# Retention attention into a gated two-layer product on one core: the last block's first product as seven products, in turns with the block before it

## The chip, the cores and the metric

The kernel runs on one core of a Trainium2 chip. The metric is the device time of one execution in microseconds, as a median over runs. The profile is one more execution, recorded by the hardware profiler. Its engines are TensorE (PE, with its weight loads shown apart as PEld), VectorE (DVE), ScalarE (ACT), GpSimd (POOL) and SyncE (SP), which here issues nearly all DMAs. TensorE writes to PSUM, which has eight banks of 2 KB per partition; the other results go to SBUF.

## What is computed

The first part is a causal attention without softmax, whose scores decay with distance by a factor of each head; the second is two matrix products with a gate between them. There are 8 batches, 8 heads, 576 positions, a head size of 64, a model width of 512 and an inner width of 2048:

```python
scores = scale * np.matmul(q, k.transpose(0, 1, 3, 2))
Dmat = np.where(rel >= 0, gamma[:, None, None] ** rel[None, :, :], 0.0)
x = np.matmul(scores * Dmat[None, :, :, :], v)   # then (batch, position) rows x 512
h = x @ w_in                                     # 4608 x 512 by 512 x 2048
g = h * (1.0 / (1.0 + np.exp(-beta * h)))        # beta: one value per inner column
out = g @ w_out                                  # 4608 x 2048 by 2048 x 512
```

## The kernel before

The 4608 rows are worked on in nine blocks of 512. Blocks 0 to 7 are the first 512 positions of each batch; block 8 collects the last 64 positions of the eight batches, the tails. The attention of a block leaves its rows turned in `xT` (width on the partitions). The first product (`up`, L761) makes one of 16 stripes of 128 inner columns with four matmuls of 128x512; ScalarE applies Silu with the column's `beta` to it out of PSUM. From block 3 on the odd stripes go through an f32 scratch (`hs`), and VectorE scales them by a ratio of betas (L773), so that two neighbouring stripes have the same scale. The sixteen stripes together are `gT`.

From block 3 on the second product is made by a scheme of seven products for a 2x2 splitting of both factors, instead of eight. The sums of `gT` quarters that it needs are made by VectorE (`seven_a`, L783: `sa`), in two halves of eight stripes; those of the weights were made once (`seven_b`). Each product and each half of the rows is one chain of eight matmuls of 128x256 (`seven_mm`, L794). The products run in the order 3, 4, 1, 5, 2, 7, 6 on three PSUM chains: U takes 3, then 2 and 6 on top; W takes 4, then 5; Z takes 1, then 7. What stands in a chain after each product is taken out at once (`seven_out`, L810): after 4, ScalarE copies W to c12 and VectorE adds U to it for c21; after 1, ScalarE copies Z to c22; after 5, ScalarE copies W to c11 and VectorE makes c12 = c21 - c11; after 2, VectorE subtracts U from c21; after 7, it adds Z to c11; after 6, U to c22. A product that is added to a chain must wait until the chain's last state has been read.

The order of work is written by hand, and each engine works through its own queue in the order in which the program issues instructions. `fill` is a list of steps, mostly TensorE's: for every block from 3 on 16 `up` and then 14 `seven_mm` (seven products, two halves of the rows). All other work (loads, preparation on POOL, turning by DMA, attention, sums) lies in `streams` of pairs (position, step). `merged` (L913) issues each of them just ahead of the fill entry with that number. `base[n]` is the number of block n's first entry; a position below is called a slot, counted from the block's start. The loop at L1101 places the sums `seven_a`, the loop at L1114 the attention: in the turn of block n the attention of block n + 1.

The tails' attention lies in the turn of block 7. `pair_prep` places its loads (`load_tail`), its preparation on POOL (`pre`) and its turning (`x_tail`, a transposing DMA on SP) by distances to two anchors. `tail_scores` (L701) is placed at slot 5, and `both_tails` (L754) at slot 13: it makes the outputs and then the parts that come from the states, behind a fence on ScalarE. The last step of the tails is `out` (L747): four times two casts of 128x256 on ScalarE from PSUM to block 8's `xT`, at slots 16.3 to 22.5.

PSUM tiles share their banks by tags: "mm" has three, "O" and "sc" two each, "st" one. The tiles of `up` take "mm" in turn, and so do the chains U and W; Z takes "O". Attention scores and outputs take "sc" and "O". For the last block each half of the rows has chains of its own (`alone`), which take further banks of "sc".

Of the kernel before, what the change touches and what calls it, by code (L numbers as in the profile page):

```python
# [19 lines left out]
def kernel(  # L20
# [10 lines left out]
    nc = tc.nc  # L31
# [703 lines left out]
    def tail_crosses(i0, later):  # L735

        O4, after = live[i0]["O4"]

        def cross(j, x, t, y, pp, after):
            p = 2 * y + pp  # L740
            mm(O4[x, y][row_d(j ^ y), pp, t, :], ends[2 * t + x][row_d(j), p, :], live[i0 + t]["qkT"][row_d(j), 0, p, half(x)],
               after=after)

        for own in range(2):
            paired(*[[F(cross, j, j ^ own, t, y, pp, after if own else None) for t in range(NT) for pp in range(2) for y in range(2)]
                     for j in range(2)])
        def out(x, y, O):  # L747
            for r in range(2):
                to = xt(B)[:, 2 * y:2 * y + 2].rearrange("k p (a r) (s l x) -> k (p a) r l x s", r=2, l=2, x=2)[:, :, r, :, x, :]
                nc.scalar.copy(to, O[:].rearrange("k p (a l) (r s) -> k (p a) r l s", l=2, r=2)[:, :, r])  # L750

        later += [F(out, x, y, O) for (x, y), O in O4.items()]
# [23 lines left out]

    def quarter(m, odd, second, ks):

        return gts[m][:, 2 * ks.start:2 * ks.stop].rearrange("f (k j) (p i) s -> f k j p i s", j=2, i=2)[:, :, odd, :, second]
# [14 lines left out]
    def seven_mm(m, j, p, alone):  # L794

        c, n = chain_of[j], p if alone else 0
        if j in (3, 4, 1) and (alone or p == 0):
            tag = {"U": ("mm", "mm"), "W": ("mm", "sc"), "Z": ("O", "sc")}[c][p] if alone else "O" if c == "Z" else "mm"
            chains[c, n] = psum.tile([P, 1 if alone else 2, NH], F32, name=c, tag=tag, bufs=dict(mm=3, O=2, sc=2)[tag])
        for k in range(KH):  # L800
            if j in (3, 4):
                a = gts[m][:, 2 * k + (j == 4), 2 * p + (j == 4), :]
            else:
                a = sums_a[0][:, held_in[j], k, p, :]
            nc.tensor.matmul(chains[c, n][:, 0 if alone else p], a, sevens[k // 2][:, j - 1, k % 2, :],  # L805
                             start=j in (3, 4, 1) and k == 0 and (alone or p == 0), stop=k == KH - 1, skip_group_check=True)
        if alone or p == 1:
            seven_out(m, j, slice(p, p + 1) if alone else slice(0, 2), n)
# [31 lines left out]
    def seven_store(m, a, ps, ns):  # L840

        for p in range(ps.start, ps.stop):
            if m < B:
                nc.sync.dma_start(out[m * S:m * S + MB].rearrange("(s i) n -> s i n", i=CB)[:, 2 * p + a, ns], ots[m][:, 2 * p + a, ns])
            else:
                rows = out.rearrange("(b s) n -> s b n", s=S)[MB + a * TL // 2:MB + (a + 1) * TL // 2, CB * p:CB * (p + 1), ns]
                nc.sync.dma_start(rows, ots[m][:, 2 * p + a, ns])

# [245 lines left out]
    lead[B - 1] = 5  # L1094
# [6 lines left out]
    for n in range(SB, B + 1):  # L1101
# [5 lines left out]
        else:  # L1107
            early = [t + 11.4, t + 12.6, t + 15.3, t + 15.4] if n == SB + 1 else [t + 9.8, t + 10.8, t + 11.8, t + 14.4] if n < B else span(t + 9, 4)
# [5 lines left out]
    for n in range(1, B):  # L1114
# [65 lines left out]
```

## Time and profile before

| What | us |
|---|---|
| median of 3 runs (lowest to highest) | 292.71 (291.99 to 292.92) |
| the profiled execution | 293.46 |
| its span, first to last instruction | 291.8 |
| block 7, first product, with the tails' scores and outputs | 234.04 to 249.91 |
| block 7, second product | 249.91 to 262.35 |
| block 8, first product | 262.35 to 275.95 |
| block 8, second product | 275.95 to 288.4 |
| last combination and stores | 288.4 to 291.8 |

All times inside the span are counted from its start. A row of a group or of a timeline names the line of the kernel, the engine, the operation, the tile written and the tiles read, and the shape; in square brackets stand the idle time of the engine ahead of it and what ended that. Matmuls overlap in TensorE's pipeline, so a matmul's own duration (273 ns for 256 columns) is longer than the distance between two of them.

### The profile page before, as it was taken

How to read it: one execution, taken by the hardware profiler on the slowest of the kernel's cores; microseconds unless marked ns; L12 is line 12 of the kernel's file. 1: busy time of each engine (PE TensorE's matmuls, PEld its weight loads, DVE VectorE, ACT ScalarE, POOL GpSimd, SP SyncE). 2: the span in 40 equal slices, each digit the busy share in tenths (PEclk: the TensorE clock that was granted, in tenths of full speed). 3: DMA queues.
4: the chain of work that ended last, by engine and by line, in shares of the span. 5: the costliest groups of instructions: out<-in, count | busy, mean ns of one | idle time of the engine just before them, and what ended most of it. 6: DMA issues, size and time to landing. Idle time of an engine off the chain costs nothing.

```text
span 291.8 us, 8653 instructions
## 1 busy us (share of the span) xinstructions
PE 280.2 (96%) x3599; PEld 177.4 (61%) x3627; DVE 187.6 (64%) x347; ACT 169.5 (58%) x298; POOL 133.0 (46%) x258
## 2 busy tenths in 40 slices
PE   7899999999999999999999899999999999999995
PEld 5674446764544455548845685578557855784584
DVE  5974545704795296299598794986498545642673
ACT  4377636686968873674157514762476156837730
POOL 6366029924980972678583593434079300000000
PEclk9999999999999999999999999999999999999999
DMA  7999999969999999999999928960678530003004
GB/s 223 309 365 385 380 306 283 189 127 239 186 196 284 222 163 260 283 234 162 255 258 182 246 62 231 175 141 2 205 163 171 81 146 3 0 24 122 0 3 143
DMA packets 120568, 54.05 MB, mean 185 GB/s; under 512 B 93889, under 2 KB 113361, under 8 KB 120529
## 3 DMA queue, kind: packets, MB, share of 16 engines
q1 hardware_dynamic: 120496, 53.49, 76.5%
q8 instruction: 28, 0.46, 0.6%
q14 instruction: 12, 0.09, 0.1%
q10 hardware_dynamic: 32, 0.01, 0.0%
HBM read 36.71 MB, written 9.44 MB: 158 GB/s over the span
## 4 chain that ended last, share of the span: by engine, by line
PE 88%; DVE 5%; DMA 3%; issue 2%; SPq 1%; ACT 0%; POOL 0%; DVEq 0%
PE ph L768 37%; PE po L893 14%; PE U L805 10%; PE Z L805 7%; PE W L805 6%; PE O L550 4%; PE ph L860 4%; DMA kvn<-in_k_dram 3%; PE sc L550 2%; DVE sa L789 2%; PE st L550 2%; DVE sbd L293 1%; PE ph L875 1%; DVE sum L586 1%; PE st L510 1%
## 5 line engine op out<-in xcount | busy, mean ns | idle before, releaser
L768 PE MATMUL ph<-xT,w_in_sb 128*128 128x512 bf16 (+1 forms) x542 | 114.2, 363 | 2.2 <-issue 0.6
L768 PEld LDWEIGHTS <-w_in_sb 128*128 128x128 bf16 x560 | 53.5, 98 | 56.1 <-DVE sum L586 0.9
L775 ACT ACTIVATE gT<-ph,beta_sb 128x512 bf16<-128x512 f32 (+1 forms) x92 | 58.3, 640 | 44.5 <-PE ph L768 43.5
L805 PEld LDWEIGHTS <-sa 128*128 128x128 bf16 x480 | 46.9, 98 | 6.3 <-issue 0.6
L773 DVE TENSOR_SCALAR gT<-hs,ratio 128x512 bf16<-128x512 f32 x48 | 25.8, 539 | 34.4 <-ACT hs L772 33.9
L789 DVE TENSOR_TENSOR sa<-gT 128x1024 bf16<-128x1024 bf16 (+1 forms) x54 | 44.5, 866 | 0.7 <-PE Z L805 0.4
L330 POOL TENSOR_TENSOR qs<-qn,gq 128x256 bf16<-128x256 f32 x48 | 31.9, 696 | 28.1 <-DMA qn<-in_q_dram 20.8
L772 ACT ACTIVATE hs<-ph,beta_sb 128x512 f32<-128x512 f32 x48 | 33.0, 687 | 20.0 <-PE ph L768 19.7
L893 PE MATMUL po<-w_out_sb,gT 128*128 128x512 bf16 x184 | 42.0, 379 | 1.0 <-issue 0.8
L312 POOL TENSOR_TENSOR vn<-kvn,gv 128x256 bf16<-128x256 f32 x48 | 33.3, 714 | 7.6 <-issue 3.2
L367 POOL CAST kn<-kvn 128x128 bf16<-128x128 f32 (+1 forms) x72 | 25.0, 383 | 17.2 <-DMA kvn<-in_k_dram 17.1
L893 PEld LDWEIGHTS <-gT 128*128 128x128 bf16 x192 | 18.1, 98 | 20.9
L805 PE MATMUL U<-b,sa 128*128 128x256 bf16 x192 | 22.9, 273 | 0.4 <-DVE ot L819 0.4
L805 PE MATMUL Z<-b,sa 128*128 128x256 bf16 x192 | 23.1, 273 | 0.0
L293 DVE TENSOR_TENSOR R<-sc,late 128x512 bf16<-128x512 f32 x24 | 15.4, 679 | 11.2 <-issue 10.0
L805 PEld LDWEIGHTS <-gT 128*128 128x128 bf16 x192 | 18.7, 98 | 3.5
L255 DVE TENSOR_TENSOR b<-wt 128x512 bf16<-128x512 f32 x20 | 15.9, 851 | 1.9 <-ACT wt L238 1.8
L448 DVE TENSOR_TENSOR R<-sc,causal 128x512 bf16<-128x512 f32 x16 | 10.2, 682 | 2.2 <-PE sc L550 2.0
L379 POOL CAST kn<-kvn 128x512 bf16<-128x512 f32 x6 | 3.8, 653 | 16.9 <-DMA kvn<-in_k_dram 16.9
L805 PE MATMUL W<-b,gT 128*128 128x256 bf16 x96 | 11.5, 273 | 0.0
L805 PE MATMUL W<-b,sa 128*128 128x256 bf16 x96 | 11.5, 273 | 0.0
L805 PE MATMUL U<-b,gT 128*128 128x256 bf16 x96 | 11.5, 273 | 0.0
(121 smaller groups left out, 316.7 us busy)
## 6 DMA issues: line engine op xcount, KB each, us to landing
qn<-in_q_dram SPq DMA_DIRECT2D x16, 512.0 KB, 5.6
out_dram<-ot SPq DMA_DIRECT2D x32, 256.0 KB, 3.2
wt<-in_moe_w_out_dram SPq DMA_DIRECT2D x8, 512.0 KB, 9.4
kvn<-in_k_dram SPq DMA_DIRECT2D x12, 256.0 KB, 6.6
kvn<-in_v_dram SPq DMA_DIRECT2D x12, 256.0 KB, 5.9
kvn<-in_k_dram SPq DMA_DIRECT2D x24, 128.0 KB, 4.7
kvn<-in_v_dram SPq DMA_DIRECT2D x24, 128.0 KB, 3.8
wt<-in_moe_w_in_dram SPq DMA_DIRECT2D x5, 512.0 KB, 8.3
```

The source lines that it names most:

```text
L293: return lambda: f(*a)
L312: nc.gpsimd.tensor_tensor(vn[:, hs], v[:, hs], g[:, hs], ALU.mult)
L330: nc.gpsimd.tensor_tensor(batch[b]["qs"][:, cs, to], q_tiles[b][:, hs, cs].rearrange("p h i d -> p i h d"), gq[:, cs, hs].unsqueeze(3).to_ ...
L367: nc.gpsimd.tensor_copy(kn[:, c % 2, to], t[:, 0, hs])
L550: ins = nc.tensor.matmul(out, lhsT, rhs, start=start, stop=stop, skip_group_check=True)
L768: nc.tensor.matmul(ph, w_in_sb[:, ko, fo * P:(fo + 1) * P], xts[m][:, ko, :, w], start=(ko == 0), stop=(ko == KO - 1))
L772: nc.scalar.activation(h, ph, ACT.Silu, scale=beta_sb[:, fo:fo + 1])
L773: nc.vector.tensor_scalar(gts[m][:, fo], h, ratio[:, fo // 2:fo // 2 + 1], None, ALU.mult)
L775: nc.scalar.activation(gts[m][:, fo, :, w], ph, ACT.Silu, scale=beta_sb[:, fo:fo + 1])
L789: nc.vector.tensor_tensor(sums_a[0][:, held_in[j], ks], quarter(m, *x, ks), quarter(m, *y, ks), op)
L805: nc.tensor.matmul(chains[c, n][:, 0 if alone else p], a, sevens[k // 2][:, j - 1, k % 2, :], start=j in (3, 4, 1) and k == 0 and (alone o ...
L893: nc.tensor.matmul(po[:, :nn], gT[:, fo, ms, :], w_out_sb[:, fo, n0:n0 + nn], start=(fo == 0), stop=(fo == FO - 1))
```

## The change

Block 8's sixteen `up` steps leave the fill list. Block 8's first product is now made by the same kind of scheme with seven products, transposed: the weights `w_in` are the operand that stays in TensorE, and the block's rows stream by. `w_sums` makes the five sums of weight quarters on POOL (20 steps of 128x512 bf16), in two halves from 11 slots before block 7's start on. `x_sums` makes the five sums and two negations of the rows' quarters at slots 10 to 16 of block 7, the sums on VectorE and the negations on ScalarE. `up_seven(g, j)` issues product j for group g (four of the sixteen stripes) in two halves `q`, four matmuls of 128x256, and then the same kind of combination as `seven_out`, on f32 tiles `cs` of 128x512. The chains are `chain8`: two U in the banks of "sc", one W in "st", one Z in "O". `swish8` applies Silu from those tiles; the odd stripes are scaled by POOL, or by VectorE in the last of the four groups.

`down_and_up(7)` takes the place of block 7's 14 `seven_mm` steps: each is split in two halves of four matmuls, and behind each of the first 24 halves stands one product of block 8 (two at the start of a group). Two halves with what stands behind them are one entry of `fill`, so the mixed stage has 14 entries, and `base[8]` counts as if 16 ended with them. The banks of two of the `alone` chains of block 8's second product change places.

The tails' scores move to slot 0.3, which is issued ahead of entry 1, their outputs to 5.6, their casts to 6.4, 6.5, 8.3 and 8.4, two of the four now on VectorE; their loads, preparation and turning move eight slots earlier with them. Block 8's sums `seven_a` are spread anew.

```diff
-        def out(x, y, O):
+        def out(n, x, y, O):
             for r in range(2):
                 to = xt(B)[:, 2 * y:2 * y + 2].rearrange("k p (a r) (s l x) -> k (p a) r l x s", r=2, l=2, x=2)[:, :, r, :, x, :]
-                nc.scalar.copy(to, O[:].rearrange("k p (a l) (r s) -> k (p a) r l s", l=2, r=2)[:, :, r])
+                e = nc.vector.tensor_copy if n % 2 else nc.scalar.copy
+                e(to, O[:].rearrange("k p (a l) (r s) -> k (p a) r l s", l=2, r=2)[:, :, r])
...
-    def seven_mm(m, j, p, alone):
+    def seven_mm(m, j, p, alone, ks=range(KH)):
...
-            tag = {"U": ("mm", "mm"), "W": ("mm", "sc"), "Z": ("O", "sc")}[c][p] if alone else "O" if c == "Z" else "mm"
+            tag = {"U": ("mm", "sc"), "W": ("mm", "mm"), "Z": ("O", "sc")}[c][p] if alone else "O" if c == "Z" else "mm"
...
+    def w_sums(ks):
+        w = w_in_sb[:].rearrange("p (r o) (k e f) -> p r o k e f", r=2, e=2, f=P)
+        cols = slice(ks.start * P, ks.stop * P)
+        def one(j):
+            if j not in ws:
+                ws[j] = stage.tile([P, KO // 2, KH * P], BF16, name="ws", tag="kvn", bufs=NQ)
...
+            for o in range(KO // 2):
+                to = ws[j][:, o, cols].rearrange("p (k f) -> p k f", f=P)
+                nc.gpsimd.tensor_tensor(to, *[w[:, r, o, ks, e] for e, r in (x, y)], op)
+        return [F(one, j) for j in (1, 5, 2, 7, 6)]
...
+    def up_seven(g, j):
+        c = chain_of[j]
+        if not chain8:
+            gts[B] = [stage.tile([P, KH, CB, P], BF16, name="g8", tag="qn", bufs=2) for _ in range(2)]
+            for k, tag, n in (("U0", "sc", 2), ("U1", "sc", 2), ("W", "st", 1), ("Z", "O", 2)):
+                chain8[k] = psum.tile([P, 2, 2 * P], F32, name="c8", tag=tag, bufs=n)
...
+        for q in range(2):
+            k = 2 * g + q
+            for o in range(KO // 2):
+                a = w[:, o if j == 3 else 2 + o, k, int(j == 4)] if j in (3, 4) else ws[j][:, o, k * P:(k + 1) * P]
+                nc.tensor.matmul(t[:, q], a, xs[j][:, o], start=j in (3, 4, 1) and q == 0 and o == 0, stop=o == KO // 2 - 1,
+                                 skip_group_check=True)
...
+        if j == 4:
+            nc.scalar.copy(c12, t)
+            nc.vector.tensor_tensor(c21, c12, chain8[f"U{g % 2}"][:].rearrange("f q (p s) -> f q p s", p=2), ALU.add)
+        elif j == 1:
+            nc.scalar.copy(c22, t)
+        elif j == 5:
+            nc.scalar.copy(c11, t)
+            nc.vector.tensor_tensor(c12, c21, c11, ALU.subtract)
+        elif j == 2:
+            nc.vector.tensor_tensor(c21, c21, t, ALU.subtract)
+        elif j == 7:
+            nc.vector.tensor_tensor(c11, c11, t, ALU.add)
+        elif j == 6:
+            nc.vector.tensor_tensor(c22, c22, t, ALU.add)
...
+        nc.scalar.activation(h, h, ACT.Silu, scale=beta_sb[:, fo:fo + 1])
+        by = nc.vector if g == WG - 1 else nc.gpsimd
+        by.tensor_scalar(gt(B, fo)[:, 0].rearrange("f i s -> f (i s)"), h, ratio[:, fo // 2:fo // 2 + 1], None, ALU.mult)
...
+    def down_and_up(m):
+        halves = [F(seven_mm, m, j, p, False, range(x * KH // 2, (x + 1) * KH // 2)) for j in seven for p in range(2) for x in range(2)]
+        units = [[f] for f in halves]
+        for g in range(WG):
+            for x, js in enumerate(((3, 4), (1,), (5,), (2,), (7,), (6,))):
+                units[6 * g + x] += [F(up_seven, g, j) for j in js]
+            for x, e, q in ((5, 0, 0), (6, 0, 1), (6, 1, 0), (7, 1, 1)):
+                units[6 * g + x].append(F(swish8, g, e, q))
...
-        base[n] = len(fill)
-        fill += [F(up, m, fo) for fo in range(FO)]
+        base[n] = len(fill) - (FO if m == B else 0)
+        fill += [F(up, m, fo) for fo in range(FO)] if m < B else []
+        if m == B - 1:
+            fill += down_and_up(m)
+            continue
...
-    lead[B - 1] = 5
+    lead[B - 1] = -3
...
+            if n == B:
+                order = [(t + 12, 5, first), (t + 13, 2, first), (t + 14.1, 7, first), (t + 16.1, 1, first)]
+                order += [(t + 16.8 + 0.1 * x, j, second) for x, j in enumerate((1, 5, 2, 7))] + [(t + 22.1, 6, first), (t + 22.2, 6, second)]
...
-            streams.append([(t0, F(tail_scores, take[0])), (t + 13, F(both_tails, take[0], outs))] +
-                           queued([t + 16.3, t + 17.6, t + 20.5, t + 22.5], outs))
+            streams.append([(t + 0.3, F(tail_scores, take[0])), (t + 5.6, F(both_tails, take[0], outs))] +
+                           queued([t + 6.4, t + 6.5, t + 8.3, t + 8.4], outs) +
+                           [(t + 10 + x, F(x_sums, j)) for x, j in enumerate((3, 4, 1, 5, 2, 7, 6))])
+            streams.append(queued(span(t - 11, 5, 2.4), w_sums(slice(0, KH // 2))) + queued(span(t + 2, 5, 2.4), w_sums(slice(KH // 2, KH))))
```

More of the change, by code (lines that the diff above doesn't have):

```diff
@@ new lines, in x_sums @@
+    def x_sums(j):
+        if not xs:
+            for n, tag in enumerate(("kn", "kn", "kT", "kT")):
+                t = sb.tile([P, 2, KO // 2, 2, P], BF16, name=tag, tag=tag, bufs=4)
+                xs.update({1 + 2 * n: t[:, 0], 2 + 2 * n: t[:, 1]})
+        x = xts[B][:].rearrange("k (r o) (p i) s -> k r i o p s", r=2, i=2)
+        b11, b12, b21, b22 = (x[:, r, i] for r in range(2) for i in range(2))
+        if j in (2, 5):
+            for o in range(KO // 2):
+                nc.scalar.activation(xs[j][:, o], (b11 if j == 2 else b22)[:, o], ACT.Copy, scale=-1.0)
+            return
+        l, r, op = {1: (b11, b22, ALU.add), 3: (b12, b22, ALU.subtract), 4: (b21, b11, ALU.subtract),
+                    6: (b11, b12, ALU.add), 7: (b21, b22, ALU.add)}[j]
+        nc.vector.tensor_tensor(xs[j], l, r, op)
@@ new lines, in swish8, with unit @@
+    def swish8(g, e, q):
+        fo, h = 4 * g + 2 * q + e, cs[g % 2][e][:, q]
+        if e == 0:
+            nc.scalar.activation(gt(B, fo)[:, 0].rearrange("f i s -> f (i s)"), h, ACT.Silu, scale=beta_sb[:, fo:fo + 1])
+            return
+        nc.scalar.activation(h, h, ACT.Silu, scale=beta_sb[:, fo:fo + 1])
[9 more added lines that the diff above has]
+                units[6 * g + x].append(F(swish8, g, e, q))
+        def unit(n):
+            for f in units[2 * n] + units[2 * n + 1]:
+                f()
+        return [F(unit, n) for n in range(len(units) // 2)]
```

28 lines of the change are left out of this document (22 added, 6 removed).

## The prediction

> **What bounds the kernel now.** I read the busy table first, then the chain that ended last, then the busy time by stages, and last the timelines of single engines around the last two blocks. Busy table, two lines of the chain, and four stages (columns: stretch, length, then busy time of PE, PEld, DVE, ACT, POOL with instruction counts, granted clock, DMA share, GB/s):
>
> ```profile
> PE 280.2 (96%) x3599; PEld 177.4 (61%) x3627; DVE 187.6 (64%) x347; ACT 169.5 (58%) x298; POOL 133.0 (46%) x258
> ...
> 250.07 1.75 PE U L805 x16
> ...
> 276.11 1.75 PE U L805 x16
> ...
> 160.50:162.50 2.00, 0.90 (x61) 0.68 (x50) 1.55 (x4) 0.00 (x0) 0.85 (x2) 1.00 0.63 97
> ...
> 234.04:249.91 15.87, 15.62 (x253) 7.82 (x255) 8.59 (x16) 10.46 (x16) 0.00 (x0) 1.00 0.17 64
> 249.91:262.35 12.44, 12.39 (x113) 11.06 (x113) 7.25 (x12) 7.13 (x13) 0.00 (x0) 1.00 0.02 8
> 262.35:275.95 13.60, 13.54 (x62) 6.17 (x63) 6.58 (x12) 10.28 (x15) 0.00 (x0) 1.00 0.19 71
> ```
>
> The reader is to see that TensorE (PE) sets the end: in the last three stages it never waits, while VectorE (DVE) is half idle and ScalarE (ACT) idles in the second product (7.13 of 12.44 us). So a change here gains only TensorE work, and loses wherever it makes TensorE wait. The prices of the other engines come from the timelines (start, length, engine, line, tiles, idle time before):
>
> ```profile
> 238.80 2.48 DVE L717 TENSOR_TENSOR R<-sc,tri 128x512 bf16<-128x512 f32 x4
> 251.35 2.50 DVE L789 TENSOR_TENSOR sa<-gT 128x1024 bf16<-128x1024 bf16 x4
> 262.34 0.69 DVE L833 TENSOR_TENSOR ot<-ot,U 128x512 f32<-128x512 f32 x1 [1.06 <-PE U L805]
> 250.11 0.69 ACT L772 ACTIVATE hs<-ph,beta_sb 128x512 f32<-128x512 f32 x1 [0.18 <-PE ph L768]
> 250.70 2.44 ACT L750 CAST xT<-O 128x256 bf16<-128x256 f32 x4
> 255.35 0.59 ACT L821 COPY ot<-Z 128x512 f32<-128x512 f32 x1
> 255.83 1.31 ACT L750 CAST xT<-O 128x256 bf16<-128x256 f32 x2
> 164.26 5.80 DVE L789 TENSOR_TENSOR sa<-gT 128x1024 bf16<-128x1024 bf16 x6
> 170.71 1.91 PE L805 MATMUL U<-b,sa 128*128 128x256 bf16 x16 [0.43 <-DVE ot L819]
> ```
>
> To see here: a Silu takes 0.69 us, but the next ScalarE step starts 0.59 behind it; a 128x512 copy takes 0.59 and frees the engine after 0.48; an output cast of the tails costs 0.61 to 0.65; a VectorE combination out of PSUM 0.69 (0.62 in a row: the four masks); a sum of 128x1024 costs 0.62 in a row. The last two lines are block 4: six sums in a row kept VectorE for 5.80 us, the read of U stood behind them, and TensorE waited 0.43. That is how this change can lose.
>
> **The change part by part.**
>
> *TensorE.* From the U chain of block 7 to that of block 8 (250.07 to 276.11) are 26.04 us. A seven-product chain of 16 matmuls takes 1.747 (starts 249.91, 251.66, 253.40), so 109.2 ns for 256 columns and 12.23 us for block 7's 112. The other 13.81 us are block 8's 64 matmuls of 512 columns, 215.8 ns each. Removed: 64 x 0.2158 = 13.81. Added: 4 groups x 7 products x 4 = 112 matmuls of 256 columns x 0.1092 = 12.23. Gain 1.58 us; the mixed stage then needs 24.46 of pure TensorE time.
>
> *Tail attention eight slots earlier* (scores from slot 5 to slot 1 of block 7, outputs from 13 to 6; a slot is one entry of the fill list). TensorE does the same 0.67 + 1.56 us. Scores end at 235.6, the four masks 2.48 later at 238.1; outputs come at 239.9: no wait. All else of the tails moves along: 24 loads and 4 transposes on SP, 32 POOL steps. On SP the first tail's six loads (189.52 to 194.4, 4.9 us) now stand ahead of the last key transpose of batch 7, whose scores run at about 206, with 3.4 us to land: hidden by some 8 us, and up to 4.9 without that. The second tail's loads pass block 5's first stores, which wait on VectorE until 204 anyway: nothing. The last transposes, issued until 227.9 before, move to about 221, for scores at 234.9. POOL ends the tails by about 222 instead of 228.8; the last tail's values there may wait for batch 7's outputs (217.5), with only the new weight sums queued behind. Each of these is costed at nothing.
>
> *Weight sums on POOL.* 20 steps of 128x512. No row has bf16 operands; the nearest is the value scaling of 128x512 at 1.04 us, bounds 0.65 (the cast of that size) and 1.81 (two of 128x256 at 0.906). At 1.04: 222 to 243; at 1.81: 258. The first ten are wanted at 253 and are done by 240 even then, the second at about 265: hidden. The upper end would slow block 7's sums beside it (six at 0.97 while POOL worked, against 0.62), some 1.4 us.
>
> *ScalarE in block 7's first product.* Block 7's 16 Silus now share their stage with four of the eight output casts, which before lay in ScalarE's free time, and four negations (0.3 each: half of the 0.62 of a 128x512 negation). Walk with 0.863 us per `up`: `up` 6 ends at 242.31; Silu 6, two casts, Silu 7 at 244.17, Silu 8 at 244.77, two casts, Silu 9 at 246.63, ready 247.32. Three PSUM buffers serve the `ph` tiles, so `up` 12 needs that one: due at 246.63, it starts at 247.37. **0.75 us lost.** Bounds: 0 if casts cost 0.37 (a plain 128x256 copy), 1.3 if no two steps overlap. I take 0.75, by the rows of the same casts. The stage ends at T = 250.82; the last Silu starts at T + 0.6.
>
> *The mixed stage.* Per group (g) ScalarE has four Silus and three copies (4 x 0.59 + 3 x 0.48 = 3.8 us), VectorE five combinations (3.3), TensorE 6.12: by totals all fits. Four groups and block 7's own 5 combinations and sums take VectorE to about 24 of 24.5, so it is the order that decides. First group: VectorE ends block 7's first-product work and the input sums at T + 2.7, reads U for c21 until 3.4, then has block 7's four second-half sums (2.5) in front of c12 = c21 - c11 (to 6.5) and c21 -= U (to 7.15). TensorE wants to add product 6 into U at T + 5.25 and starts at 7.2: **1.95 lost** (bounds 1.35, if the input sums are done early, and 2.6, if every step takes its full length). For the next groups the loop is: VectorE c11 += Z; ScalarE four Silus, then copies c12, block 7's own, c22, c11, queued behind the Silu that waits; VectorE c12 and c21. That is 4 x 0.6 + 4 x 0.5 + 0.1 and three times 0.65: 6.5 us against 6.12. In group 2 (and 3, 4) I get waits of **0.85, 1.2 and 0.6** at product 6; group 3 has block 7's sum of 128x2048 (1.23) in its way, group 4 two first-half sums of block 8. Together 2.65; bounds 0 (loop below 6.12) and 4.7 (the same walk with every step at full length).
>
> *Block 8's second product.* TensorE has T + 29.1 for its first chain, 30.85 for its second (W), whose PSUM buffer is that of block 7's U. That is read last by block 7's c22 += U, which stands on VectorE behind two multiplications that wait for the last Silus and one sum: done at 32.5. **1.7 lost**; after it sums and chains keep up. Bounds 0.5 (Silus 1.2 earlier) and 2.5.
>
> *Nothing* I put on the rest: stores, the halves of chains (same matmuls), and the multiplications that go to POOL. The last are 0.65 to 1.04 each, in the 6.5 us of a group, and are wanted two groups later; if they fell beside c12, that one would take 1.10 (172.12, POOL busy) instead of 0.69.
>
> Sum: -1.58 + 0.75 + 1.95 + 2.65 + 1.7 = +5.5 us. The profiled execution took 293.46 (span 291.8 and 1.66 around it), 0.75 above the median of the three runs, 292.71; it would come to 298.9, the median to **298.2**. All low ends together +0.3 (293.0), all high ends +9.5 (302.2).
>
> **Rivals.**
>
> *Evictions keep up* (other side). Place: the read of U before product 6 of each group; price: all waits go, 292.71 - 1.58 = 291.1. It decides where the group loop falls below 6.12 us and the first group's chain ends by T + 5.25. For: no second product of blocks 5 to 7 waits, and totals fit. Against: the first chain holds 2.5 us of sums that no overlap shortens. If only some of the waits go, the gain and they cancel: 291.8 to 293.6, no change.
>
> *The change doesn't save TensorE time.* Every 256 columns need a weight load of 98 ns, inside 109; with two streams in turns, a load not taken ahead at a switch would cost 98 ns, 56 switches 5.5 us: 303.7. Against: U, W and Z chains follow each other now with other tiles and banks at an even 1.747.
>
> *The clock drops.* The waits come in every group. In block 4 TensorE stood still for 0.94 us and the stretch from 160.50 kept the clock at 1.00. If the clock halved for one group's 56 matmuls, that is 6.1 us more, 304.3. The Trainium skill, page TensorE: Matmul & The Clock Gate, section "A second HAM failure mode: psum-queue depth-cycling", says that short idle gaps between groups as banks are cycled can throttle the clock. The trace shows no such thing; its gaps were fewer than those I expect.
>
> **How the numbers follow.** The forecast 0.74 (293.6 to 302.2); evictions keep up 0.13; waits and gain cancel 0.05; no TensorE saving 0.05; clock 0.03. The point is the forecast's, 298.2. The range leaves out the faster case, the clock and half of the unsaved time (0.19): 292.0 to 302.2; the forecast's own is 293.6 to 302.2. A measurement of this kernel tells about 0.3% (0.9 us) from no change: faster 0.13, same 0.05, slower 0.82.
>
> **What would show it.** The matmul work of the last two blocks falls by about 1.6 us, at 109 ns a step within groups. Block 7's first product takes about 16.8 us instead of 15.9, its late Silus back to back. TensorE waits for VectorE's subtraction from U before each product 6, first for about 2 us; the mixed stage takes 29.1. A wait of about 1.7 us for block 7's last combination stands before block 8's W chain. POOL's sums end by about 243, and the clock stays 1.00. I am wrong if the mixed stage takes under 26 us, if VectorE's four sums do not stand between c21 and c12, or if TensorE waits for POOL or a transpose.

## The result and the profile after

The changed kernel takes 303.05 us (median of six runs, 301.82 to 304.15); the kernel before took 292.46 beside it (291.99 to 293.05). The ratio is 1.034 with a 95% interval of 1.032 to 1.037: slower, by nearly twice what was forecast, and just above the range. The profiled execution took 302.85 with a span of 300.8, so the spans are 9.0 us apart. The medians are 10.6 apart: the profiled execution of before (293.46) is 1.0 above its median, that of after 0.2 below, and some 0.4 lies outside the spans. Two matmuls are missing in the profile of before, the first `up` of block 6 and that of block 7, so that its rows begin at 205.23 and 234.04 (the figure used ahead of the result). The starts used here, 205.02 and 233.83, are the ends of the chains before, 16 x 0.1092 = 1.75 us behind their starts. Taken apart at the same points of the two TensorE timelines:

| Stretch | before, us | after, us | predicted | measured |
|---|---|---|---|---|
| start to block 6's first `up` | 205.02 | 203.97 | 0 | -1.05 |
| block 6, both products | 28.81 | 33.04 | 0 | **+4.23** |
| block 7, first product | 16.08 | 16.50 | +0.75 | +0.42 |
| first U chain of block 7 to that of block 8 | 26.04 | 29.64 | +3.0 | +3.60 |
| from there to the start of block 8's last U chain | 10.48 | 11.19 | +1.7 | +0.71 |
| from there to the end | 5.37 | 6.46 | 0 | +1.09 |

The first row is scatter: with the tails moved in the same way, this stretch took between 204.0 and 205.8 us in the profiles below. The forecast's places are there, with 4.7 us together where 5.45 was expected. What it missed is 4.2 us in block 6, a block before the one that is rebuilt. Two lines of the page, the busy table and the group of the weight sums:

```profile
PE 283.6 (94%) x3675; PEld 182.7 (61%) x3675; DVE 205.0 (68%) x371; ACT 172.2 (57%) x310; POOL 166.7 (55%) x284
...
L869 POOL TENSOR_TENSOR ws<-w_in_sb 128x512 bf16<-128x512 bf16 x20 | 26.8, 1381 | 0.0
```

TensorE's busy time rises although its matmul work falls, and VectorE's rises by 17.4 us. What TensorE waited for from 200 us on (us in total, times, longest):

```profile
PE c L904 <- DVE c L918: 2.7, 2, 1.4
PE U L811 <- DVE ot L825: 2.0, 1, 2.0
PE c L904 <- DVE hs L918: 1.9, 2, 1.1
PE W L811 <- DVE ot L839: 0.5, 1, 0.5
PE ph L769 <- ACT hs L773: 0.3, 1, 0.3
```

Lines one and three are the four waits before product 6, line four the wait of block 8's W chain, line five ScalarE's lateness in block 7's first product: all were in the forecast. Line two was not. It stands in block 6; VectorE and GpSimd around it (timelines: start, length):

```profile
226.25 1.64 DVE L795 TENSOR_TENSOR sa<-gT 128x1024 bf16<-128x1024 bf16 x1
227.82 1.64 DVE L795 TENSOR_TENSOR sa<-gT 128x1024 bf16<-128x1024 bf16 x1
229.38 0.67 DVE L825 TENSOR_TENSOR ot<-ot,U 128x512 f32<-128x512 f32 x1
231.47 1.63 DVE L830 TENSOR_TENSOR ot<-ot 128x512 f32<-128x512 f32 x1
...
225.75 1.60 POOL L869 TENSOR_TENSOR ws<-w_in_sb 128x512 bf16<-128x512 bf16 x1
227.30 1.60 POOL L869 TENSOR_TENSOR ws<-w_in_sb 128x512 bf16<-128x512 bf16 x1
228.86 1.60 POOL L869 TENSOR_TENSOR ws<-w_in_sb 128x512 bf16<-128x512 bf16 x1
```

The two engines go in step: VectorE's sums start 1.57 us apart and GpSimd's 1.55 to 1.56, where a sum costs VectorE 0.62 on its own. The read of U (L825) stands behind four of them. It takes its usual 0.67, with one operand in PSUM; the subtraction L830, with both in SBUF, takes 1.63 instead of 0.69. VectorE's scalings from SBUF to SBUF (L774) are held up too: 0.49 on their own, and 1.37 for the last one ahead of the four sums.

```profile
221.84 1.37 DVE L774 TENSOR_SCALAR gT<-hs,ratio 128x512 bf16<-128x512 f32 x1
```

In the kernel before, the same four sums took half as long:

```profile
223.36 3.13 DVE L789 TENSOR_TENSOR sa<-gT 128x1024 bf16<-128x1024 bf16 x4
```

TensorE's timeline, with the idle time before a chain in brackets, shows what this wait cost, and then the four waits of the mixed stage:

```profile
226.15 1.91 PE L811 MATMUL W<-b,sa 128*128 128x256 bf16 x16
230.10 2.70 PE L811 MATMUL U<-b,sa 128*128 128x256 bf16 x16 [2.04 <-DVE ot L825]
232.59 2.83 PE L811 MATMUL Z<-b,sa 128*128 128x256 bf16 x16
...
260.25 0.60 PE L904 MATMUL c<-kT,ws 128*128 128x256 bf16 x4 [1.34 <-DVE c L918]
266.88 0.60 PE L904 MATMUL c<-kT,ws 128*128 128x256 bf16 x4 [0.80 <-DVE hs L918]
274.07 0.60 PE L904 MATMUL c<-kT,ws 128*128 128x256 bf16 x4 [1.35 <-DVE c L918]
280.98 0.60 PE L904 MATMUL c<-kT,ws 128*128 128x256 bf16 x4 [1.07 <-DVE hs L918]
```

The idle time in brackets leaves out the 0.16 us in which the pipeline empties. Counted from start to start, the first wait is 230.10 - 226.15 - 16 x 0.1092 = 2.20 us, and the four of the mixed stage are 1.49, 0.95, 1.51 and 1.23, together 5.18. Then 24.46 + 5.18 = 29.64, which is the stage: the matmuls themselves take just the time that the forecast gave them.

The two chains behind the first wait last 2.70 and 2.83 instead of 1.91. The windows around them and of the last stages (columns as in the prediction):

```profile
228.00:230.00 2.00, 0.06 (x1) 0.00 (x0) 2.00 (x3) 0.58 (x1) 2.00 (x2) 1.00 0.00 0
231.00:232.00 1.00, 1.00 (x8) 0.73 (x6) 1.00 (x2) 0.00 (x0) 1.00 (x1) 0.53 0.00 0
232.00:233.00 1.00, 1.00 (x6) 0.71 (x5) 1.00 (x1) 0.00 (x0) 1.00 (x2) 0.50 0.00 0
233.00:234.00 1.00, 1.00 (x7) 0.74 (x5) 0.79 (x2) 0.00 (x0) 1.00 (x1) 0.50 0.00 0
234.00:235.00 1.00, 1.00 (x9) 0.79 (x8) 0.00 (x0) 0.00 (x0) 1.00 (x2) 0.77 0.00 0
...
237.00:253.50 16.50, 16.20 (x258) 7.92 (x256) 12.87 (x21) 12.27 (x23) 9.89 (x9) 1.00 0.18 66
260.00:283.15 23.15, 19.68 (x176) 17.18 (x176) 16.63 (x25) 14.54 (x26) 10.47 (x6) 1.00 0.01 1
```

About a microsecond after TensorE resumed, the granted clock fell to 0.50 for some 3.4 us; six to seven matmuls a microsecond run there instead of eleven. U and Z lost 0.74 and 0.92 us by it. With the 2.20 that makes 3.86 of block 6's 4.23; another 0.35 lies in the chains of W and Z just ahead. In the mixed stage, with VectorE idle for a quarter of the time, the clock stays at 1.00.

### The profile page after: what moved, and what is told of

The parts are those of the page before. It is cut to its first block, busy times and chain, and to the rows that moved or that the text cites. A ratio compares the mean times of both kernels' runs of the same rounds, so it can differ in the third digit from the quotient of the medians.

```text
span 300.8 us, 8869 instructions
## 1 busy us (share of the span) xinstructions
PE 283.6 (94%) x3675; PEld 182.7 (61%) x3675; DVE 205.0 (68%) x371; ACT 172.2 (57%) x310; POOL 166.7 (55%) x284
## 4 chain that ended last, share of the span: by engine, by line
PE 79%; DVE 9%; issue 4%; ACT 3%; DMA 3%; SPq 1%; POOL 0%; DVEq 0%
PE ph L769 30%; PE po L994 14%; PE U L811 9%; PE Z L811 6%; PE W L811 5%; PE O L550 4%; PE ph L961 3%; DVE sa L795 3%; DMA kvn<-in_k_dram 3%; PE c L904 2%; PE sc L550 2%; PE st L550 2%; DVE gT L774 1%; ACT g L928 1%; ACT gT L776 1%
## 5 line engine op out<-in xcount | busy, mean ns | idle before, releaser
L769 PE MATMUL ph<-xT,w_in_sb 128*128 128x512 bf16 (+1 forms) x496 | 102.8, 362 | 0.9 <-ACT hs L773 0.3
L769 PEld LDWEIGHTS <-w_in_sb 128*128 128x128 bf16 x496 | 47.2, 98 | 49.0 <-issue 1.1
L776 ACT ACTIVATE gT<-ph,beta_sb 128x512 bf16<-128x512 f32 (+1 forms) x84 | 52.8, 636 | 41.6 <-PE ph L769 40.9
L330 POOL TENSOR_TENSOR qs<-qn,gq 128x256 bf16<-128x256 f32 x48 | 29.8, 654 | 30.1 <-DMA qn<-in_q_dram 26.0
L795 DVE TENSOR_TENSOR sa<-gT 128x1024 bf16<-128x1024 bf16 (+1 forms) x45 | 39.2, 911 | 0.5 <-PE Z L811 0.3
L774 DVE TENSOR_SCALAR gT<-hs,ratio 128x512 bf16<-128x512 f32 x40 | 25.0, 628 | 20.3 <-ACT hs L773 20.1
L367 POOL CAST kn<-kvn 128x128 bf16<-128x128 f32 (+1 forms) x72 | 26.9, 411 | 17.6 <-DMA kvn<-in_k_dram 17.6
L773 ACT ACTIVATE hs<-ph,beta_sb 128x512 f32<-128x512 f32 x40 | 27.5, 688 | 16.0 <-PE ph L769 16.0
L994 PEld LDWEIGHTS <-gT 128*128 128x128 bf16 x192 | 18.1, 98 | 20.8
L869 POOL TENSOR_TENSOR ws<-w_in_sb 128x512 bf16<-128x512 bf16 x20 | 26.8, 1381 | 0.0
L811 PEld LDWEIGHTS <-gT 128*128 128x128 bf16 x160 | 15.5, 98 | 3.2 <-DVE gT L774 0.3
L932 POOL TENSOR_SCALAR g<-c,ratio 128x512 bf16<-128x512 f32 x4 | 6.2, 1566 | 19.1 <-ACT c L930 19.1
L379 POOL CAST kn<-kvn 128x512 bf16<-128x512 f32 x6 | 3.8, 652 | 16.1 <-DMA kvn<-in_k_dram 16.1
```

The costliest lines, as they stand in the source:

```text
L330: nc.gpsimd.tensor_tensor(batch[b]["qs"][:, cs, to], q_tiles[b][:, hs, cs].rearrange("p h i d -> p i h d"), gq[:, cs, hs].unsqueeze(3).to_ ...
L367: nc.gpsimd.tensor_copy(kn[:, c % 2, to], t[:, 0, hs])
L769: nc.tensor.matmul(ph, w_in_sb[:, ko, fo * P:(fo + 1) * P], xts[m][:, ko, :, w], start=(ko == 0), stop=(ko == KO - 1))
L773: nc.scalar.activation(h, ph, ACT.Silu, scale=beta_sb[:, fo:fo + 1])
L774: nc.vector.tensor_scalar(gts[m][:, fo], h, ratio[:, fo // 2:fo // 2 + 1], None, ALU.mult)
L776: nc.scalar.activation(gts[m][:, fo, :, w], ph, ACT.Silu, scale=beta_sb[:, fo:fo + 1])
```

## The experiments

**1. The tails alone.** The kernel before with the tails' attention, their preparation and their casts as in the change (two of the four casts on VectorE); everything else as before.

```diff
-    lead[B - 1] = 5
+    lead[B - 1] = -3
...
-            streams.append([(t0, F(tail_scores, take[0])), (t + 13, F(both_tails, take[0], outs))] +
-                           queued([t + 16.3, t + 17.6, t + 20.5, t + 22.5], outs))
+            streams.append([(t + 0.3, F(tail_scores, take[0])), (t + 5.6, F(both_tails, take[0], outs))] +
+                           queued([t + 6.4, t + 6.5, t + 8.3, t + 8.4], outs))
```

> The kernel before with one part of the change: the tails' loads, preparation, turning, scores, outputs and casts at their new, earlier places (two of the four casts on VectorE); block 8's first product is made by sixteen up steps as before, and there are no weight sums. Theory P (the weight sums on POOL slow VectorE's sums in block 6): block 6 takes 28.8 us as before, block 7's first product 0 to 0.8 us more, TensorE's clock stays 1.00, the median is 292.3 to 293.5. Rival H (the tails' earlier loads, preparation and turning are what disturbs block 6): block 6 takes about 33 us, the median is 296 to 298.

Measured: 293.63 against 292.61, ratio 1.003 (1.001 to 1.004). Block 6 took 28.80 us, as before; block 7's first product 16.50 instead of 16.08, which is all that the changed kernel lost there. Where the rest of the 1.0 us in the median lies isn't known. The tails are not what slowed block 6.

**2. The tails and the weight sums.** The same with GpSimd's 20 sums at their places; nothing uses them.

```diff
+            streams.append(queued(span(t - 11, 5, 2.4), w_sums(slice(0, KH // 2))) + queued(span(t + 2, 5, 2.4), w_sums(slice(KH // 2, KH))))
```

> e1 with the twenty weight sums on POOL added where the change has them; nobody reads them. Theory P: block 6's sums of 128x1024 take about 1.6 us each while POOL works, TensorE waits about 2 us for VectorE in block 6, its clock falls for some us behind that wait, and the median is 3.5 to 5.5 us above that of e1 (296 to 298.5). Rival H, or sums that are hidden as I had forecast: as e1, within 0.9 us.

Measured: 298.43 against 292.61, ratio 1.019 (1.016 to 1.022). The sums alone cost 4.8 us over experiment 1, and block 6 took 33.6. Three of its four runs show a mean granted clock of 0.994 and took 298.37 to 298.50; the fourth shows 1.000 and took 296.63, about as much less as U and Z lost by the clock above. Its timelines repeat the changed kernel's:

```profile
224.68 6.20 DVE L795 TENSOR_TENSOR sa<-gT 128x1024 bf16<-128x1024 bf16 x4
...
231.53 2.33 PE L811 MATMUL U<-b,sa 128*128 128x256 bf16 x16 [2.04 <-DVE ot L825]
```

**3. The change without the sums.** The weight quarter itself goes into products 1, 5, 2, 7 and 6 in place of the sum, and GpSimd's sums are left out.

```diff
-                a = w[:, o if j == 3 else 2 + o, k, int(j == 4)] if j in (3, 4) else ws[j][:, o, k * P:(k + 1) * P]
+                a = w[:, o if j == 3 else 2 + o, k, int(j == 4)]
```

> The changed kernel without the weight sums: all products of block 8's first product take a quarter of the weights itself in their place, so block 8's result is not the product; matmuls, evictions and all else are the same. Theory P: block 6 is back to about 28.8 us, the clock stays 1.00, the mixed stage keeps its four waits for VectorE (1.0 to 1.4 us each), and the median falls by 4 to 6 us, to 297 to 299. Rival H or hidden sums: no change, 302 to 304.

Measured: 298.93 against 292.61, ratio 1.022 (1.021 to 1.024), some 4 us under the changed kernel. Block 6 is back at 28.83 us and its wait is gone; the four waits of the mixed stage are the same to 0.01 us. The four sums on VectorE, and TensorE's waits:

```profile
223.00 2.50 DVE L795 TENSOR_TENSOR sa<-gT 128x1024 bf16<-128x1024 bf16 x4
...
PE c L904 <- DVE c L918: 2.7, 2, 1.4
PE c L904 <- DVE hs L918: 1.9, 2, 1.1
```

So the loss is made of two parts that do not touch each other: the sums in block 6, and the order of evictions in the mixed stage.

**4. Copies in place of the sums.** GpSimd copies one weight quarter (one operand) where it added two.

```diff
-                nc.gpsimd.tensor_tensor(to, *[w[:, r, o, ks, e] for e, r in (x, y)], op)
+                nc.gpsimd.tensor_copy(to, w[:, x[1], o, ks, x[0]])
```

> The changed kernel with each weight sum on POOL replaced by a copy of one of its two quarters (128x512 bf16, same places, so block 8's result is not the product). If it is POOL steps with two inputs that slow VectorE: VectorE's sums in block 6 stay at about 0.8 to 1.0 us, block 6 takes under 30 us, the median is 297.5 to 299.5. If any POOL step does it as long as it runs: sums of about 1.6 us beside the copies, but for a shorter time (20 copies of 0.4 to 0.65 us, 8 to 13 us against 26.8), block 6 takes 30 to 32 us, the median 299.5 to 302.

Measured: 298.22 against 292.61, ratio 1.022 (1.017 to 1.028); block 6 28.79, without a wait. GpSimd's and VectorE's rows:

```profile
219.52 15.30 POOL L869 COPY ws<-w_in_sb 128x512 bf16<-128x512 bf16 x20
...
222.21 4.02 DVE L795 TENSOR_TENSOR sa<-gT 128x1024 bf16<-128x1024 bf16 x4
```

Beside the sums GpSimd's copies start 1.01 us apart, elsewhere some 0.58 (231 us); VectorE's sums come every 1.00. In the changed kernel the pair takes 1.56, and GpSimd's two-operand step alone 1.12 (three in 3.37 from 234.07 on). In both cases that is GpSimd's own time and 0.42 to 0.44 of VectorE's 0.62. So both kinds of GpSimd step slow VectorE's sums, each by its length less about 0.2 us. Neither of the two expectations had this quite: one-operand steps do slow VectorE, but only for as long as they themselves last. With copies the read of U ended at 226.82, some 0.8 us before the chain that waits for it began (227.59).

**5. The sums on VectorE.** The ten sums of 128x1024 lie in VectorE's idle gaps of blocks 6 and 7.

```diff
-                nc.gpsimd.tensor_tensor(to, *[w[:, r, o, ks, e] for e, r in (x, y)], op)
+            nc.vector.tensor_tensor(to, *[w[:, r, o, :, e] for e, r in (x, y)], op)
...
+            streams.append(queued([t - 29.5] * 4 + [t - 7.8, t - 5.9, t - 3.9, t - 1.9, t + 0.2, t + 2.5], w_sums()))
```

> The changed kernel with the weight sums on VectorE instead of POOL, ten steps of 128x1024 placed where VectorE idles in blocks 6 and 7. Theory P: block 6 takes 28.8 to 29.4 us, the clock stays 1.00, the rest is as in e3 (four waits in the mixed stage, 4.6 us together); the median is 298 to 299.8. If VectorE has no room for them, block 6 or block 7's first product grows by up to 6 us, and the median stays at 302 or above.

Measured: 298.69 against 293.11, ratio 1.018 (1.015 to 1.021); block 6 took 28.95. The cost of the sums is gone, the waits of the mixed stage stay (1.34, 0.79, 1.35, 1.07 of idle time).

**6. Block 7's own sums later.** Experiment 5, and the four second-half sums that stood before the first group's c12 are spread over the next entries.

```diff
+            if n == B - 1:
+                halves += [(t + 17.5, 1, second), (t + 18.5, 5, second), (t + 20.5, 2, second), (t + 21.5, 7, second),
+                           (t + 23.5, 6, first), (t + 24.5, 6, second)]
```

> e5, and block 7's four second-half sums and its sum for product 6 (in two halves) are issued later, spread over the groups instead of in one lot behind the first group's c21. Theory Q (the waits of the mixed stage come from the order on VectorE's and ScalarE's queues): the first group's wait of 1.34 us goes to 0.3 or less, the others stay within 0.5 of what they were; the median falls by 0.7 to 1.6 us against e5. Rival T (VectorE's total work is the limit: about 24 us in 24.5): the first wait goes but comes back in later groups, the median within 0.5 us of e5.

Measured: 298.79 against 293.11, ratio 1.019 (1.015 to 1.022): no gain. That is what the rival had forecast, that VectorE's total work is the limit. The first group's wait went from 1.49 to 0.23, and new ones came in its place:

```profile
260.07 0.60 PE L902 MATMUL c<-kT,ws 128*128 128x256 bf16 x4 [0.43 <-ACT hs L908]
263.66 0.60 PE L902 MATMUL c<-kT,ws 128*128 128x256 bf16 x4 [0.81 <-DVE hs L916]
```

The mixed stage still took 29.6 us. Moving the sums alone is not enough: ScalarE's copies come too late as well. Whether that is for want of time or for their order, this run can't tell; experiment 9 can.

**7. Groups that overlap.** Experiment 6, and product 6 of a group is issued among the next group's products, the Silus one or two entry halves later, c12 is formed from PSUM, and block 8's first sums come later.

```diff
+            if g:
+                units[6 * g].append(F(up_seven, g - 1, 6))
...
-            nc.vector.tensor_tensor(c12, c21, c11, ALU.subtract)
+            nc.vector.tensor_tensor(c12, c21, t, ALU.subtract)
```

> e6, and in addition: c12 is made from W in PSUM and not from the copy of it; product 6 of each of the first three groups is issued after the next group's first half of block 7, and their Silus behind the next group's copies; three of block 8's first-half sums are issued after the last group. Theory Q: the waits in the mixed stage sum to less than 1 us (the matmuls then take 24.5 to 25.5), the wait in block 8 is under 0.6; the median is 293.5 to 295.5. Rival T: at least 2.5 us of waits remain, the median is 296 or above.

Measured: 297.26 against 293.11, ratio 1.013 (1.010 to 1.016). Waits of under 1 us were expected; there were still three, 3.7 us together, and the stage took 28.6, again what the rival had forecast. VectorE shows why:

```profile
267.53 0.69 DVE L914 TENSOR_TENSOR qs<-c,c 128x512 f32<-128x512 f32 x1 [1.62 <-ACT qs L913]
274.90 0.69 DVE L914 TENSOR_TENSOR hs<-hs,c 128x512 f32<-128x512 f32 x1 [1.38 <-ACT hs L913]
```

The subtraction no longer reads ScalarE's copy, but it is still issued behind it and still waits for it, while the copy stands in ScalarE's queue behind Silus.

**8. All small repairs.** Experiment 7, with the casts spread, the negations on GpSimd, and block 7's stores in halves as they become ready.

```diff
-        if m == B and j in (5, 2, 7, 6):
+        if m >= B - 1 and j in (5, 2, 7, 6):
...
+            nc.gpsimd.tensor_scalar(xs[j], b11 if j == 2 else b22, -1.0, None, ALU.mult)
```

> e7, and in addition: the tails' casts are spread (first and last pair on ScalarE, at slots 6.4 and 10.9, the middle ones on VectorE), the two negations go to POOL, and block 7's stores leave in halves after products 5, 2, 7 and 6. If block 7's first product lost 0.6 us to the casts, it takes 15.9 to 16.1 us again; if the end lost 1.1 us because block 7's stores come just ahead of block 8's, it takes 5.4 to 5.6 us from the last U chain's start instead of 6.4. Both together: the median 1 to 2 us under e7, 291.5 to 294. If neither is the cause: as e7.

Measured: 296.86 against 293.11, ratio 1.012 (1.008 to 1.015). ScalarE's wait in block 7's first product is gone (16.1 us, as in the kernel before); the earlier stores did not shorten the end (6.5 us from the last U chain on). The median fell by 0.4 us against experiment 7, where 1 to 2 were expected.

**9. c12 before the copy.** Experiment 8, with VectorE's subtraction issued ahead of ScalarE's copy of the same tile, and the Silus of the first three groups behind the next group's copies.

```diff
-            nc.scalar.copy(c11, t)
             nc.vector.tensor_tensor(c12, c21, t, ALU.subtract)
+            nc.scalar.copy(c11, t)
```

> e8, with two edits to ScalarE's order: VectorE makes c12 from W before ScalarE copies W to c11 (in e8 it still stood behind that copy, 0.9 to 1.4 us idle), and the four Silus of each of the first three groups are issued behind the next group's three copies, the odd stripes first. Theory Q (order, not totals): the waits of the mixed stage fall from 3.7 us to 0.8 or less, the mixed stage from 28.8 to 25 to 26 us, the median by 2.4 to 3.4 us against e8, to 293.4 to 294.5. Rival T (totals of VectorE and ScalarE): at least 2.5 us of waits stay, the median 296 or above.

Measured: 295.25 against 292.61, ratio 1.008 (1.005 to 1.011). The mixed stage fell from 28.8 to 25.96 us with the same steps on every engine. The median missed its forecast (293.4 to 294.5): in these profiles 1.0 of the 2.85 us is lost again in block 8's second product, where TensorE waits for ScalarE's last Silus and then for VectorE (11.52 us up to its last U chain instead of 10.48), and 0.7 at the end. One long wait of the stage is left (first line TensorE's waits). Ahead of the step that it waits for (L915, at 268.05) VectorE stands idle twice, first for GpSimd's scalings, then in block 7's own c12 (L830) for ScalarE's copy of the same tile:

```profile
PE c L901 <- DVE c L915: 0.9, 1, 0.9
...
264.82 0.69 DVE L908 TENSOR_TENSOR c<-qs,c 128x512 f32<-128x512 f32 x1 [1.31 <-POOL g L929]
...
267.44 0.69 DVE L830 TENSOR_TENSOR ot<-ot 128x512 f32<-128x512 f32 x1 [1.14 <-ACT ot L829]
```

So it was the order of the evictions and not their amount. Two edits were made at once, the subtraction and the Silus; which of them did how much isn't separated. Block 7's c12 is still made from ScalarE's copy.

**10. The last stores.** Experiment 9, and half of block 8's stores are issued by ScalarE.

```diff
-                nc.sync.dma_start(rows, ots[m][:, 2 * p + a, ns])
+                (nc.scalar if (a, ns.start) in ((0, 0), (1, NH)) else nc.sync).dma_start(rows, ots[m][:, 2 * p + a, ns])
```

> e9, with block 8's last four stores (after products 7 and 6) issued by ScalarE's queue, which is idle by then, instead of SP's. In e8 SP's issue of the fourth of these eight stores took 1.6 us where its others took 0.6, and the last one left 0.95 us after its data were ready. If this is what the end costs, the time from the last U chain's start to the end falls from 6.5 to 5.4 to 5.7 us, and the median to 0.6 to 1.1 us under e9. If the stores are slow on the way and not at issue: as e9.

Measured: 295.05 against 292.61, ratio 1.008 (1.005 to 1.011). From the last U chain's start on it took 5.6 us in the profile instead of 7.2, and the median span fell by 0.6 us (293.35 to 292.75), but the median time by 0.2 only: no gain that can be told.

**11. The changed kernel with that edit alone.**

> The changed kernel itself with that one edit: block 8's last four stores issued by ScalarE. If the late issue on SP is what the end of the changed kernel costs (6.5 us from the last U chain's start, 5.4 before the change): 5.4 to 5.7 us, the median 302.0 to 302.5, 0.6 to 1.1 us less. Otherwise as the changed kernel, 303.05.

Measured: 302.75 against 292.61, ratio 1.034 (1.031 to 1.036); the changed kernel took 303.05. No difference that can be told, and not the 302.0 to 302.5 that was expected, though the end took 5.3 us in the profile instead of 6.5. This profile has something else to show. It has the same wait in block 6, and no fall of the clock behind it (TensorE's timeline, and two windows):

```profile
231.63 1.91 PE L811 MATMUL U<-b,sa 128*128 128x256 bf16 x16 [2.04 <-DVE ot L825]
...
232.00:233.00 1.00, 1.00 (x12) 0.90 (x10) 1.00 (x1) 0.00 (x0) 1.00 (x1) 1.00 0.00 0
233.00:234.00 1.00, 1.00 (x11) 0.90 (x10) 1.00 (x2) 0.00 (x0) 1.00 (x1) 1.00 0.00 0
```

The other three runs of this kernel had mean clocks of 0.992 to 0.994 and took 0.3 to 0.9 us longer, but a mean does not say where the clock fell. So the wait is in all three profiles that have GpSimd's sums (after, experiments 2 and 11), and the halved clock behind it in two of them.

**12. The odd Silus earlier.** Experiment 10, with the odd stripes' Silus in ScalarE's idle gap behind the copy of product 1.

```diff
-            for x, e, q in ((9, 1, 0), (9, 1, 1), (10, 0, 0), (10, 0, 1)) if g < WG - 1 else ((5, 0, 0), (6, 0, 1), (6, 1, 0), (7, 1, 1)):
+            for x, e, q in ((7, 1, 0), (7, 1, 1), (9, 0, 0), (9, 0, 1)) if g < WG - 1 else ((5, 0, 0), (6, 0, 1), (6, 1, 0), (7, 1, 1)):
```

> The kernel with the last stores issued by ScalarE, with one more edit: in the first three groups the odd stripes' Silus are issued two entry halves earlier, behind the copy of product 1, where ScalarE stood idle for 0.97 to 1.47 us, and the even ones one half earlier. Theory Q (what is left over the kernel before is TensorE's waiting: 1.04 us for GpSimd's scalings and 1.04 us in block 8's second product for the last Silus, counted as the distance of TensorE's starts above the matmuls' own time): GpSimd starts its scalings some 1.4 us earlier, VectorE's sum of product 4 no longer waits for them, the mixed stage falls from 25.95 to about 24.9 us, the waits in block 8's second product go, and the median falls from 295.05 to 293.0 to 293.5, level with the kernel before (292.6) within 0.3%. Rival T (the work of the other engines does not fit whatever its order): the copy of W behind product 5 now stands behind the Silus, new waits of about 1 us a group take the place, and the median stays at 295.

Measured: 293.41 (12 runs) against 292.87, ratio 1.0015 (0.9994 to 1.0036): level with the kernel before, as expected. One wait of TensorE is left; GpSimd's first scalings now start 9.8 us into the stage instead of 11.3:

```profile
PE c L901 <- DVE c L915: 0.7, 1, 0.7
...
259.88 3.11 POOL L929 TENSOR_SCALAR g<-c,ratio 128x512 bf16<-128x512 f32 x2 [8.96 <-ACT c L927]
```

The mixed stage took 25.55 us (24.9 was expected): 24.46, that wait with 0.91 and a gap of 0.18. That is 0.49 less than in the kernel before. Block 8's second product up to its last U chain took 10.48, exactly as before. Of the 0.49, 0.06 is given back in block 6 and block 7's first product (44.95 us instead of 44.89, with the weight sums and the tails in it) and 0.21 at the end (5.58 instead of 5.37). What is left, 0.2 us, is too little to show in the medians. GpSimd's wait ahead of that subtraction is gone, yet TensorE's fell only from 1.04 to 0.91: VectorE still stands idle 1.29 us for ScalarE's copy in block 7's c12. The edit of experiment 9 was not tried there. No version tried beats the kernel before.

## Why the prediction was wrong

**The step that failed** is "*Weight sums on POOL*", and in it the words "the second at about 265: hidden". The sums were in time for TensorE, as that step argued, but it asked only when they were wanted. It named the harm ("the upper end would slow block 7's sums beside it"), priced it at 1.4 us, tied it to the longer duration and put it in block 7. It came at a step of 1.12 us, close to the middle estimate of 1.04, and in block 6, where four sums stand before the read of U; with copies of 0.58 TensorE did not wait. Of VectorE's steps it was the ones with no operand in PSUM, the sums, subtractions and scalings; the scaling and the sum ahead of the four made those start 2.70 us behind the start of the first U chain instead of 1.44 (experiment 3). Experiments 2, 3 and 5 show it: 4.8 us with the sums added, some 4 gone with the sums left out or moved. The sign was in the prediction's own lines of block 4: six sums at 0.97 us beside GpSimd's work, and 0.43 us of TensorE's waiting behind them.

The Trainium skill has the rule, on the page SBUF — State Buffer, section "SBUF: two separate sides": GpSimd and VectorE share a port pair that a GpSimd step, or a VectorE step with two SBUF inputs or in a mode that uses both ports, holds for the whole instruction while the other blocks. The trace agrees in the main: the two engines went in turns, one sum of each every 1.56 us, and the VectorE steps with an operand in PSUM kept their 0.67. By that rule the four sums would cost 4 x (1.12 + 0.62) = 7.0 us, an estimate from durations of the trace; the trace has 6.2, some 0.2 less each time. There the measurement decides.

**"The clock stays 1.00"** failed with it: the 2.20 us wait, which the forecast did not have, was followed by 3.4 us at half clock, 1.66 us in the profiled execution. The rival on the clock had a halving right, but neither its place nor its price (6.1 us): it expected it from the repeated waits of the mixed stage, where four waits of 0.95 to 1.51 us left the clock at 1.00. The page TensorE: Matmul & The Clock Gate of the Trainium skill (Part 1, "What's actually happening") gives free-running windows of about 3.4 us. The length of the drop, and that experiment 11's profile has none behind the same wait, fit such a window. The page asks for a whole idle window before the clock falls; the wait here was 2.2 us, and there the measurement decides. Why the clock fell behind this wait in some executions only stays open.

**TensorE's saving** was right: between the waits, the mixed stage runs at 109 ns a step, 24.46 us in all. The rival without that saving is out.

**The mixed stage** was right in mechanism and nearly in size: waits of 1.95, 0.85, 1.2 and 0.6 were forecast, 1.49, 0.95, 1.51 and 1.23 were measured; 4.6 against 5.18. The place was right, VectorE's late subtraction from U before product 6. The reason given for the first holds: four sums stand between c21 and the next subtraction (VectorE's timeline in the changed kernel), and with most of them moved (experiment 6) that wait fell to 0.23.

```profile
255.72 0.68 DVE L911 TENSOR_TENSOR c<-qs,c 128x512 f32<-128x512 f32 x1
256.32 2.49 DVE L795 TENSOR_TENSOR sa<-gT 128x1024 bf16<-128x1024 bf16 x4
258.73 0.68 DVE L916 TENSOR_TENSOR qs<-c,qs 128x512 f32<-128x512 f32 x1
259.51 0.69 DVE L918 TENSOR_TENSOR c<-c,c 128x512 f32<-128x512 f32 x1
```

But the time of the stage stayed, as other waits took its place. Experiments 7 to 12 show what held the loop: the order among ScalarE's copies, the Silus and VectorE's c12.

**ScalarE in block 7's first product**: 0.42 against 0.75, and all of it comes with the tails alone (experiment 1). **Block 8's W chain**: 0.72 (286.49 - 284.90 - 8 x 0.1092) against 1.7, but within the bounds. VectorE ended the last combination (L839) 1.53 us behind the chain's start, about as forecast (1.65), but the chain's first eight matmuls did not wait for it:

```profile
284.90 1.04 PE L811 MATMUL W<-b,g 128*128 128x256 bf16 x8
286.49 1.03 PE L811 MATMUL W<-b,g 128*128 128x256 bf16 x8 [0.55 <-DVE ot L839]
```

**The tails' move at nothing** was nearly right: 1.0 us in the median of experiment 1, 0.42 of it the lateness of ScalarE just named, and none of it in block 6.

**Stores and end at nothing** were wrong by 1.1 us. One store of block 8 took SyncE 1.92 us to issue where the others took some 0.64, and the last left 1.1 us after its data were ready.

```profile
293.89 1.92 SPq L853 DMA_DIRECT2D out_dram<-ot  x1
```

The profiled end took 5.7 to 7.2 us in the changed versions whose stores SyncE issues, and 5.3 to 5.6 in the kernel before, in experiments 1 and 2 and with half of the stores on ScalarE's queue; but the medians show no gain from that (experiments 10 and 11). Why one issue takes so long in these kernels stays open.

**Evictions keep up**, the rival on the faster side, was not what the change does. Experiment 12 comes near its condition, and still only ties.

## What to carry to other kernels

Before work goes to an idle GpSimd, look at what VectorE does beside it: each of its steps with no operand in PSUM can then last nearly as long as it and the GpSimd step together (1.56 us for 0.62 and 1.12 here), so read in VectorE's queue which eviction stands behind them and how much slack it has. Where products are added into chains that must be read out first, totals by engine say little; follow the reading of each chain through both eviction queues, and issue the step that frees the bank ahead of everything that nobody waits for.

## What the runs showed of the hardware

- VectorE's bf16 sum of 128x1024 takes 0.62 us alone, 1.00 beside GpSimd's one-operand copies (0.58 alone) and 1.56 in lockstep with its two-operand sums (1.12 alone). A scaling of 128x512 from SBUF to SBUF took 1.37 there instead of 0.49; steps with one operand in PSUM kept 0.67.
- One TensorE wait of 2.2 us was followed by some 3.4 us at half clock in two of three profiles, and by none in the third; the four waits of 0.95 to 1.51 us in the mixed stage left the clock at 1.00.
- Of eight equal stores in a row on SyncE, one sometimes took 1.6 to 1.9 us to issue instead of some 0.64. The cause is open.
